# Block 0's rows and the queries' weights in two transfers each, biases turned by a plain matmul, outputs in new PSUM places, more tiles added in chunks 1 and 3

## The chip, the core and the metric

One core of a Trainium2 chip runs the whole program. Its engines work side by side, each through its own list of instructions: TensorE (PE, with its weight loads as PEld), VectorE (DVE), ScalarE (ACT), GpSimd (POOL) and SyncE (SP), which here only issues transfers. The metric is the device time of one execution in microseconds (us).

## What is computed

For x of 2048 rows and 640 columns, a layer norm without weights, and then two branches whose results are added to x: attention with 32 heads of 20 columns, where each row attends to itself and to seven earlier rows, two apart; and a dense layer of 1536 columns with gelu.

```python
def _A_ref(x, wqkv, wo):
    ...
    H = 32; Dh = D // H
    W, dil = 8, 2
    ...
    idx = pos[:, None] - off[None, :]
    mask = idx >= 0
    ...
    logits = jnp.einsum("bhsd,bhswd->bhsw", q, kg) * scale
    logits = jnp.where(mask[None, None, :, :], logits, -1e9)
    attn = _softmax(logits, axis=-1)
    o = jnp.einsum("bhsw,bhswd->bhsd", attn, vg)
    return ... @ wo
def _B_ref(x, w1, b1, w2, b2):
    h = _gelu(x @ w1 + b1)
    return h @ w2 + b2
xn = _layernorm(x)
return x + _A_ref(xn, A_wqkv, A_wo) + _B_ref(xn, B_w1, B_b1, B_w2, B_b2)
```

The second function is written here with `@` in place of its einsums.

## The kernel before

The rows are handled in four chunks (n = 0 to 3) of 512, each of four blocks (bl) of 128. A chunk's normalised rows are turned so that columns lie on the partitions (tile xnT). From it TensorE makes queries, keys and values (L336, in chunk 0 L349 and L380 in pieces) and the dense layer's first product (L599, tile hps), which ACT turns into hT with gelu (L615). Every product's PSUM tile comes from a pool of four banks (psA), two banks (psO) or the one place for the logits (psL, tile L).

Attention runs on VectorE. Queries times the eight shifted keys fill two big tiles, half 0 and half 1 (L433, four instructions a chunk). Each head's 20 columns lie as 4 partitions by 5 tiles; the sum over partitions is done by TensorE (L479, tile L) by a product with a 0/1 matrix, and the sum over the 5 tiles either by accumulating products in L479 or, in part, by adds on VectorE first (L465 adds pairs of tiles, L470 one tile to the first). LEVEL says how much per chunk: at 0 L479 runs 40 times, at 1 24, at 2 16, at 3 8. Then come mask (L490, chunk 0 only), maximum (L510), subtraction (L516), exponential on ACT (L526), sum (L530), reciprocal by logarithm and exponential on ACT (L538, L539), and the product with it (L544, tile attn). SP spreads attn over the partitions by transfers (L563, tiles ax or parts of x_sb), VectorE multiplies it with the shifted values (L578, eight a chunk) and adds up (L587, L592) to tile oT.

Chunks 0 to 2 leave turned: TensorE adds w2 x hT and wo x oT into tile T (L673, five slices s of 128 columns), ACT adds the bias (L676), SP turns the slice back by a transposing transfer (L680), and POOL adds it to the output in memory by an accumulating transfer (L685). Chunk 3 leaves straight, a block of rows at a time: the first 512 columns in tile lo, the other 128 in hi (L634, L636). Its blocks 0 to 2 go by ACT's copies (L641, L642) and accumulating transfers of POOL (L646); the last block is added to x by VectorE (L693, L702) and written by SP (L694) and ACT (L707). The x rows that the accumulating transfers add to were written to the output before (L301, L305).

The order is written out by hand, as one long list of names (ORDER), and each name issues a few instructions on its engines. TensorE, VectorE, ACT and SP carry out theirs exactly in that order; POOL's order follows the program too. Names: pj and pc are a projection and its copy, f1 and ge the dense product and gelu, qk L433, pa L465, pb L470, lg L479, m, mx, ex, ss, ri, at the softmax steps, xd and xs the transfers of attn, av L578, ad L587, ot L592, t a part of T, u L676, ut L680, ud L685, o the parts of lo and hi, oc and od copies and transfers of a block of chunk 3, oclo L693 with L694, ohi the hi products of the last block, ochi L702, ochd L707. The digits behind are chunk, then block or slice, then part. At the end the list reads

```
... u24 o312 ut23 o313 ud22 ud23 ot3 o320 o321
o322 o323 o324 oc32 od32 ut24 o314 oc31 od31 o300 o301 o302 o303 o304 o332 o333 o334 ud14 ohi ud24 oc30 od30 oclo ochi
ochd
```

At the start SP loads block 0 of x (L129), then the weights of queries and keys (L132), blocks 2 and 3, the values' weights and chunk 1, while ACT's queue loads block 1 and the biases (L136 to L138); ACT makes block 1's statistics (L221, L228), VectorE those of the other blocks (L209, L211). Thirteen products without use (L446) keep TensorE busy until the first transposes (L280). The two bias vectors are laid in 17 rows of a tile of 32 (b_rt) and turned by a transpose (L456, L459).

Of the kernel before, what the change touches and what calls it, by code (L numbers as in the profile page):

```python
# [11 lines left out]
ALU = mybir.AluOpType  # L12
# [17 lines left out]
LASTB = S // P - 1  # L30
WARM = 10
RB = 32
# [3 lines left out]
LEVEL = (1, 0, 2, 2)  # L36
# [6 lines left out]
tp01a gb3 tp01b tc01a tc01b gb4 gd gc0 ge tb b1 hj102 gc1 ho st02a st02 st03a hc102 gc4 st03 hj101 rs02 xn02 rs03 xn03  # L43
st10a st12a st13a st11a hc101 st12 hj100 hc100 hj200 tp02 tc02 tp03 tc03 pk st13 hj201 hc200 st11 st10 hj202 hc202
hj012 hc012 hc201 rs1 rc1 hj112 hc112 xn12 tc12 xn10 hj210 qk000 hj011 hc011 tc10 hj110 hc110 qk001 hj010 hc010 hc210
hj111 hc111 qk011 qk010 pa011 pa001 xn11 tc11 xn13 hj211 hc211 f10_5 tc13 f10_4 ge0_4 ge0_5 f10_0 ge0_0 f10_7 f10_10
pj113 pc113 pj103 pj111 ge0_10 pj101 pc111 pj114 ldx ge0_7 pa000 pc101 pa010 lg0 mask m0a ld2 pc103 pj102 pc114 pad11
su21 mx0a ex0a pj112 pc112 m0b mx0b ss0a pc102 ex0b ri0a ss0b pj100 pc100 at0a ri0b at0b pj110 pj104 pc104 pc110 xd0
qk111 f10_2 ge0_2 su22 qk100 hj212 hc212 f10_6 ge0_6 pj121 su20 f10_1 pc121 su23 ldo f11_10 ge1_10 ng2 ge0_1 sq20
f11_5 f10_11 pj122 pc122 f10_3 qk110 sq22 t040 qk101 f11_0 t000 lg1 xp0 av010 ge0_3 sq21 xs0 ge1_0 sq23 rs2 f10_8  # L50
ge0_8 t001 m1 f11_3 rc2 xn23 tc23 ge0_11 av031 t041 mx1 av021 xn20 tc20 f11_7 av011 ge1_5 ge1_7 av001 ge1_3 xp1 f10_9
t042 t002 xn21 ge0_9 tc21 pj120 xn22 tc22 av030 av000 f11_9 ge1_9 pj124 ex1 av020 ss1 pc120 pc124 pj123 pc123 ad00 ri1
t043 f11_2 t003 pj204 at1 pc204 xd1 su31 ad01 pad12 ad02 ot0 pj200 pc200 pj201 pc201 av101 xp2 pj212 su30 pc212 pj220
pj213 pc220 pc213 pj223 pc223 pj211 su33 pc211 pj203 su32 ng3 sq33 pad21 av100 sq31 pj202 f11_6 t004 u00 av110 xs1
av130 t044 av120 av131 av121 t010 av111 t011 t012 t013 u04 t020 t014 sq32 pc203 pc202 pj221 sq30 rs3 rc3 ad11 u01 ut00
ad10 ad12 t030 pj210 pc221 t031 t021 t022 ut01 ge1_2 pj214 xn33 tc33 t032 t033 t034 xn31 tc31 ge1_6 pj224 t023 t024
f11_8 ot1 pc214 pad22 pc210 qk201 qk211 qk210 xn30 tc30 f12_9 qk200 f11_1 pa210 pa201 xn32 ge1_8 u02 pa211 pa200 f11_4
ge1_1 t100 ge1_4 tc32 pj311 pc311 pb212 ud00 ud01 ge2_9 pj310 pc310 pad31 pj304 pc304 pj314 pc314 t101 pj300 pj324
pc324 ut02 pj303 f12_10 pb202 pc224 u03 pc303 xp3 pj301 pc301 xl ge2_10 pc300 f13_9 pj313 pc313 pj312 ud02 ut03 ud03
pj302 pc302 f13_6 ge3_6 pj323 lg2 pc312 qk300 m2 pc323 f11_11 ge1_11 f13_0 ge3_0 mx2 ut04 f13_11 ge3_9 ex2 pa300 ss2  # L60
qk310 ri2 at2 xs2 qk301 t130 t131 f12_1 ge2_1 ge3_11 t132 f13_10 qk311 t102 t103 f13_2 pa310 xd2 t104 pj320 pc320
f13_1 ge3_1 u10 ut10 ud10 f12_8 pa311 pa301 pb312 ge2_8 f13_8 ge3_8 t110 t133 t111 t112 t113 t114 u11 ge3_10 f12_5
pj222 pc222 pj321 pc321 pb302 lg3 av200 t134 u13 m3 av221 ge2_5 xb3 f12_11 t140 t141 t120 ut11 mx3 f12_2 ge3_2 av211
ex3 ss3 ri3 av220 ge2_2 f13_5 ge2_11 t142 t143 t121 t122 t123 f12_6 ge2_6 at3 xs3 f12_3 ge2_3 t124 u12 f12_7 pj322
ud04 av210 av201 av231 f12_0 t144 ge2_7 ge2_0 t200 av230 pc322 u14 ut12 ud11 f12_4 ge2_4 ge3_5 f13_4 ge3_4 o310 f13_7
ge3_7 t210 ad20 ad21 ad22 ot2 f13_3 t201 t202 pad32 av321 t203 ge3_3 o311 av331 ut13 av320 xd3 t204 u20 av300 ut14
ut20 ud12 ud13 t211 t212 t240 t213 t214 av311 u21 ud20 t241 t242 av310 av330 t220 t221 t222 t223 t224 u22 ut21 t243
av301 ad30 ad31 o330 o331 t230 ad32 t231 t232 t233 t234 u23 ut22 ud21 t244 u24 o312 ut23 o313 ud22 ud23 ot3 o320 o321
o322 o323 o324 oc32 od32 ut24 o314 oc31 od31 o300 o301 o302 o303 o304 o332 o333 o334 ud14 ohi ud24 oc30 od30 oclo ochi
ochd  # L70
# [4 lines left out]
def kernel(  # L75
# [45 lines left out]
    b_rt = consts.tile([RB, P], BF16, name="b_rt")  # L121
# [12 lines left out]
    load_x(0, 1)  # L134
    nc.vector.memset(x_sb[:, 1, 0:16], 0.0)
# [3 lines left out]
    load_w(0)  # L139
    load_w(1)  # L140
    load_x(2, BPC)
    load_w(2)
    load_x(BPC, 2 * BPC)
# [151 lines left out]
    def rows(n):  # L295
        cs = slice(n * BPC, min((n + 1) * BPC, LASTB))
        return cs, out_sd.rearrange("(b p) d -> p b d", p=P)[:, cs, :]
# [9 lines left out]
    def do_xl():  # L307
        nc.vector.tensor_tensor(out=x_sb[:, LASTB, :], in0=x_sb[:, LASTB, :], in1=b2bc[:], op=ALU.add)

# [144 lines left out]
    def do_tb():  # L454
        tiles["tb"] = psL.tile([P, 2 * W * P], BF16, tag="L", name="tb")
        nc.tensor.transpose(tiles["tb"][:, 0:RB], b_rt[:], ident[0:RB, 0:RB])  # L456

    def do_b1():
        nc.vector.tensor_copy(bT[:], tiles["tb"][:, 0 : FT + KT])  # L459
# [39 lines left out]

    def shifted(n, i):  # L500
        cs, width = part(n, i)
        if PARTS[n] == 1:
            return tiles["L", n][:]
        low = half[0][:].rearrange("p w t c -> p (w t c)").bitcast(F32)[:, 0 : W * P]
        return low.rearrange("p (i w c) -> p i w c", i=PARTS[n], w=W)[:, i, :, :]
# [22 lines left out]
    def do_sum(n, i):  # L528
        total = softmax_tile("sums", n, [P], F32)
        nc.vector.tensor_reduce(  # L530
            out=total[:, i, :], in_=tiles["e", n][:, i, :, :].rearrange("p w c -> p c w"), axis=AX.X, op=ALU.add
        )

    def do_recip(n, i):
        rs = get(("rs", n), lambda: smp.tile([P, PARTS[n], P // PARTS[n]], F32, tag="m", name="rs"))
        total = tiles["sums", n][:, i, :]
        table(LOG_SET)
        nc.scalar.activation(total, total, ACT.Ln)  # L538
        nc.scalar.activation(rs[:, i, :], total, ACT.Exp, scale=-1.0)  # L539

    def do_attn(n, i):
        cs, width = part(n, i)
        attn = get(("attn", n), lambda: smp.tile([P, W, P], BF16, tag="attn", name="attn"))
# [76 lines left out]
    def do_o(n, bl, pc, parts):  # L620
        cs = slice(bl * P, (bl + 1) * P)
        if pc == 0 and "lo" in parts:
            for part in ("lo", "hi"):
                pool, tag = (psA, "acc") if bl % 2 else (psO, "o")
                tiles[part, n, bl] = pool.tile([P, CH], F32, tag=tag, name=part)
        lo, hi = tiles["lo", n, bl], tiles["hi", n, bl]
# [4 lines left out]
        for k, (lhs, rhs) in enumerate(srcs):  # L631
            first, last = pc == 0 and k == 0, pc == 4 and k == len(srcs) - 1
            if "lo" in parts:
                nc.tensor.matmul(lo[:], lhsT=lhs, rhs=rhs[:, 0:CH], start=first, stop=last)  # L634
            if "hi" in parts:
                nc.tensor.matmul(hi[:, 0 : D - CH], lhsT=lhs, rhs=rhs[:, CH:D], start=first, stop=last)  # L636
# [211 lines left out]
```

## Time and profile before

| what | us |
| --- | --- |
| median of 3 runs (lowest to highest) | 210.02 (209.96 to 210.23) |
| the profiled execution, its own time | 210.03 |
| its span, first to last instruction | 208.0 |
| PE, DVE, ACT busy between 18 and 194 us | 175.5, 169.1, 113.0 |
| PE, DVE, ACT busy after 194 us | 10.8, 1.0, 2.3 |

The span is what the profiler saw of the program; the execution took 2.0 us more. The busy times of the stretches show that TensorE and VectorE are both nearly full in the middle, and that VectorE has no more work in the last 14 us. A row of a group gives line, engine, operation, what is written and read, shapes and count, and then busy time, mean length in ns and the idle time before. A row of the timeline begins with start and length; in brackets stands the idle time before it and what ended it. The clock granted to TensorE was 0.999 of full speed.

### The profile page before, as it was taken

The page shows a single profiled execution, that of the slowest core. Times are in us where ns is not written, and L with a number is a line of the kernel's source. Part 1 is how long each engine was busy: PE and PEld are TensorE (multiplying, and loading weights), DVE is VectorE, ACT ScalarE, POOL GpSimd, SP SyncE. Part 2 cuts the span into 40 slices and gives each one's busy share as a digit, 9 for nine tenths or more (in the row PEclk, how much of TensorE's full clock was granted, in tenths as well). Part 3 has the DMA queues.
Part 4 walks back from the last instruction along what each step waited for, and adds up shares of the span by engine and source line. Part 5 has one row for each costly group of instructions (what it writes and reads, how often), then busy time and mean ns, then how long its engine had stood idle before and what let it go on. Part 6 is the DMA issues. An engine that isn't in the chain of part 4 may idle for free.

```text
span 208.0 us, 2951 instructions
## 1 busy us (share of the span) xinstructions
PE 203.5 (98%) x1164; PEld 107.0 (51%) x1164; DVE 180.9 (87%) x141; ACT 127.5 (61%) x234; POOL 24.9 (12%) x37
## 2 busy tenths in 40 slices
PE   8999999999999999999999999999999999999993
PEld 3999754554445554444455544444444444445552
DVE  2598995999699999999999989999999999999201
ACT  5589968898997877877564556744658541112210
POOL 2000000000000000220020610002200402222621
PEclk9999999999999999999999999999999999999999
DMA  6994379168426075148431790086405795556753
GB/s 217 388 395 137 68 207 395 60 122 238 162 82 162 11 189 138 25 50 91 90 25 56 114 123 0 0 188 81 37 0 100 121 108 54 50 50 76 49 68 63
DMA packets 36863, 23.88 MB, mean 115 GB/s; under 512 B 24946, under 2 KB 34674, under 8 KB 36850
## 3 DMA queue, kind: packets, MB, share of 16 engines
q1 hardware_dynamic: 26320, 18.75, 34.5%
q0 software_dynamic: 8752, 2.95, 17.8%
q10 hardware_dynamic: 1778, 2.00, 2.7%
q8 instruction: 9, 0.15, 0.3%
q14 instruction: 4, 0.03, 0.0%
HBM read 10.00 MB, written 5.57 MB: 75 GB/s over the span
## 4 chain that ended last, share of the span: by engine, by line
PE 66%; DVE 21%; ACT 9%; DMA 2%; issue 1%; DVEq 0%; ACTq 0%
PE T L673 17%; PE pps L336 15%; PE hps L599 13%; PE lo L634 7%; PE gps L380 7%; DVE half L433 5%; DVE half L587 4%; DVE sums L530 3%; PE idle L446 2%; ACT L173 2%; DVE half L465 2%; DMA xnT<-xn 2%; DVE half L578 2%; ACT hT L615 2%; PE hi L636 2%; PE gps L349 1%
## 5 line engine op out<-in xcount | busy, mean ns | idle before, releaser
L599 PE MATMUL hps<-xnT,w_sb 128*128 128x512 bf16 x240 | 56.9, 379 | 0.1
L433 DVE TENSOR_TENSOR half<-qT,kT 128x5120 bf16<-128x5120 bf16 x16 | 44.3, 2820 | 1.0 <-ACT vT L400 0.7
L673 PE MATMUL T<-hT,w_sb 128*128 128x512 bf16 x180 | 43.3, 379 | 0.0
L685 POOL DMA_DIRECT2D out_dram<-x_sb x15 | 19.5, 1357 | 172.8 <-DMA x_sb<-x_sb 168.7
L599 PEld LDWEIGHTS <-w_sb 128*128 128x128 bf16 x240 | 23.3, 98 | 28.2 <-issue 1.2
L615 ACT ACTIVATE hT<-hps,bT 128x512 bf16<-128x512 f32 x36 | 24.1, 687 | 7.3 <-PE hps L599 7.2
L673 PEld LDWEIGHTS <-w_sb 128*128 128x128 bf16 x180 | 17.6, 98 | 21.1
L578 DVE TENSOR_TENSOR half<-vT,ax 128x2560 bf16<-128x2560 bf16 x16 | 23.1, 1484 | 2.4 <-PE L L479 2.4
L676 ACT ACTIVATE x_sb<-T,bT 128x512 bf16<-128x512 f32 x15 | 10.3, 687 | 23.6 <-PE T L673 23.6
L578 DVE TENSOR_TENSOR half<-vT,x_sb 128x2560 bf16<-128x2560 bf16 x16 | 22.6, 1485 | 0.0
L587 DVE TENSOR_TENSOR half<-half,half 128x5120 bf16<-128x5120 bf16 x8 | 22.3, 2820 | 0.1
L673 PE MATMUL T<-oT,wo 128*128 128x512 bf16 x75 | 18.3, 379 | 0.3 <-DVE oT L592 0.3
L336 PE MATMUL pps<-xnT,wk_sb 128*128 128x512 bf16 x75 | 18.3, 379 | 0.0
L336 PE MATMUL pps<-xnT,wv_sb 128*128 128x512 bf16 x75 | 18.3, 379 | 0.0
L336 PE MATMUL pps<-xnT,wq_sb 128*128 128x512 bf16 x75 | 18.2, 379 | 0.0
L173 ACT ACT_TABLE_LOAD x12 | 15.4, 1283 | 0.9 <-PEq L832 0.7
L465 DVE TENSOR_TENSOR half<-half 128x2048 bf16<-128x2048 bf16 x12 | 13.9, 1217 | 0.0
L336 PEld LDWEIGHTS <-wv_sb 128*128 128x128 bf16 x75 | 8.8, 117 | 7.6
L336 PEld LDWEIGHTS <-wq_sb 128*128 128x128 bf16 x75 | 8.7, 118 | 7.7 <-issue 0.4
L336 PEld LDWEIGHTS <-wk_sb 128*128 128x128 bf16 x75 | 8.8, 117 | 7.5
L263 ACT ACTIVATE xn<-x_sb,nmr,rstd 128x640 bf16<-128x640 bf16 x12 | 10.6, 916 | 3.2 <-DMA xnT<-xn 2.3
L400 ACT CAST vT<-pps 128x512 bf16<-128x512 f32 x15 | 8.5, 589 | 6.1 <-PE pps L336 6.1
(92 smaller groups left out, 241.0 us busy)
## 6 DMA issues: line engine op xcount, KB each, us to landing
w_sb<-in_B_w_dram SPq DMA_DIRECT2D x4, 960.0 KB, 10.3
ax<-attn SPq DMA_DIRECT2D x8, 256.0 KB, 4.8
x_sb<-attn SPq DMA_DIRECT2D x8, 256.0 KB, 4.6
out_dram<-x_sb POOLq DMA_DIRECT2D x15, 128.0 KB, 4.0
x_sb<-in_A_x_dram SPq DMA_DIRECT2D x1, 1280.0 KB, 6.5
out_dram<-x_sb ACTq DMA_DIRECT2D x2, 640.0 KB, 3.1
wq_sb<-in_A_wqkv_dram SPq DMA_DIRECT2D x1, 800.0 KB, 4.7
wk_sb<-in_A_wqkv_dram SPq DMA_DIRECT2D x1, 800.0 KB, 6.3
```

Source lines behind the costliest of these rows:

```text
L173: nc.scalar.preload_act_table_set(name)
L336: nc.tensor.matmul(ps[:], lhsT=wqkv_p[which][:, ti, to, :], rhs=xnT[:, ti, :], start=(ti == 0), stop=(ti == KT - 1),)
L380: nc.tensor.matmul(ps[:, to - a, :], lhsT=wqkv_p[which][:, ti, to, :], rhs=tiles["xnT", 0][:, ti, pair * 2 * P : (pair + 1) * 2 * P], star ...
L433: nc.vector.tensor_tensor(out=half[h][:, :, :, cs], in0=q[:, :, at].unsqueeze(1).to_broadcast([P, W // 2, KT, 2 * P]), in1=window(k, h, at ...
L465: nc.vector.tensor_tensor(out=even, in0=even, in1=odd, op=ALU.add)
L578: nc.vector.tensor_tensor(out=half[h][:, :, :, cs], in0=window(qkv_tile(n, 2), h, cs), in1=ax_view(n)[:, j, ws, :].unsqueeze(2).to_broadca ...
L587: nc.vector.tensor_tensor(out=a, in0=a, in1=b, op=ALU.add)
L599: nc.tensor.matmul(ps[:], lhsT=w1_sb[:, ti, ft * P : (ft + 1) * P], rhs=tiles["xnT", n][:, ti, :], start=(ti == 0), stop=(ti == KT - 1),)
L615: nc.scalar.activation(hT, tiles["hps", n, ft][:], ACT.Gelu_apprx_tanh, bias=bT[:, ft : ft + 1], scale=1.0)
L634: nc.tensor.matmul(lo[:], lhsT=lhs, rhs=rhs[:, 0:CH], start=first, stop=last)
L673: nc.tensor.matmul(ps[:], lhsT=lhs, rhs=rhs, start=pc == 0 and k == 0, stop=pc == 4 and k == len(srcs) - 1)
L685: nc.gpsimd.dma_start(dst, src, accum_op=ALU.add)
```

## The change

- Block 0 of x is loaded in two halves of 320 columns, one on SP's and one on ACT's queue; the queries' weights in two transfers, of two and of three of the five row tiles; blocks 2 and 3 now come before the keys' weights, and chunk 1 before the values'.
- The tile b_rt has 128 rows, and a plain product with the identity turns the biases.
- LEVEL is 1 in place of 0 for chunk 1, and 3 in place of 2 for chunk 3.
- The sum of the softmax is made by three halving adds, in f32, in a free part of half 0 or of attn.
- In chunk 3, block 0 and the hi parts of blocks 0 and 1 use the place of the logits; the hi parts of blocks 2 and 3 share a bank. Block 2 too is added to x by VectorE and written by SP (new names dc and dd), and the rows written beforehand are fewer by one block.
- ORDER is a new list throughout. In chunk 0 the first two L433 are followed by their adds; chunk 1 has its pa100 pa110 pa101 pa111, chunk 3 its pb304 and pb314.

Its end reads now

```
... ot3 u24 o321 o322 o323 o313 o314 o304 oc31 oc30 o324 o333 ut22 ud22 o334 dc oclo ut23 ut24 ud23
ohi od31 od30 dd ud24 ochi ochd
```

and the rest of the diff, cut to its core (its last two lines stand near the top of the kernel):

```diff
-LEVEL = (1, 0, 2, 2)
+LEVEL = (1, 1, 2, 3)
+DIRECT = 2
...
-    load_x(0, 1)
-    nc.vector.memset(x_sb[:, 1, 0:16], 0.0)
+    for eng, cs in ((nc.sync, slice(0, D // 2)), (nc.scalar, slice(D // 2, D))):
+        eng.dma_start(x_sb[:, 0, cs], x_nb[:, 0, cs])
     nc.scalar.dma_start(x_sb[:, 1, :], x_nb[:, 1, :])
     nc.scalar.dma_start(b_rt[0:FT, :], B_b1.rearrange("(t p) -> t p", p=P))
     nc.scalar.dma_start(b_rt[FT : FT + KT, :], B_b2.rearrange("(t p) -> t p", p=P))
-    load_w(0)
+    for ts in (slice(0, 2), slice(2, KT)):
+        nc.sync.dma_start(wqkv[0][:, ts, :], wqkv_v[:, ts, 0:D])
+    load_x(2, BPC)
     load_w(1)
-    load_x(2, BPC)
+    load_x(BPC, 2 * BPC)
     load_w(2)
-    load_x(BPC, 2 * BPC)
...
     def do_xl():
-        nc.vector.tensor_tensor(out=x_sb[:, LASTB, :], in0=x_sb[:, LASTB, :], in1=b2bc[:], op=ALU.add)
+        rows_ = x_sb[:, LASTB + 1 - DIRECT :, :]
+        nc.vector.tensor_tensor(
+            out=rows_, in0=rows_, in1=b2bc[:].unsqueeze(1).to_broadcast([P, DIRECT, D]), op=ALU.add
+        )
...
     def do_tb():
-        tiles["tb"] = psL.tile([P, 2 * W * P], BF16, tag="L", name="tb")
-        nc.tensor.transpose(tiles["tb"][:, 0:RB], b_rt[:], ident[0:RB, 0:RB])
+        tiles["tb"] = psL.tile([P, W, P], F32, tag="L", name="tb")
+        nc.tensor.matmul(tiles["tb"][:, 0, 0 : FT + KT], lhsT=b_rt[:], rhs=ident[:, 0 : FT + KT], start=True, stop=True)
 
     def do_b1():
-        nc.vector.tensor_copy(bT[:], tiles["tb"][:, 0 : FT + KT])
+        nc.vector.tensor_copy(bT[:], tiles["tb"][:, 0, 0 : FT + KT])
...
+    scratch = half[0][:].rearrange("p w t c -> p (w t c)").bitcast(F32)
...
+    def sums(n, i):
+
+        if PARTS[n] == 1:
+            return attn_tile(n)[:].rearrange("p w c -> p (w c)").bitcast(F32).rearrange("p (w c) -> p w c", w=W // 2)
+        room = scratch[:, W * P : W * P + W * P // 2]
+        return room.rearrange("p (i w c) -> p i w c", i=PARTS[n], w=W // 2)[:, i, :, :]
...
     def do_sum(n, i):
-        total = softmax_tile("sums", n, [P], F32)
-        nc.vector.tensor_reduce(
-            out=total[:, i, :], in_=tiles["e", n][:, i, :, :].rearrange("p w c -> p c w"), axis=AX.X, op=ALU.add
-        )
+        a, e = sums(n, i), tiles["e", n][:, i, :, :]
+        nc.vector.tensor_tensor(out=a, in0=e[:, 0 : W // 2, :], in1=e[:, W // 2 :, :], op=ALU.add)
+        for k in (2, 1):
+            nc.vector.tensor_tensor(out=a[:, 0:k, :], in0=a[:, 0:k, :], in1=a[:, k : 2 * k, :], op=ALU.add)
...
-        total = tiles["sums", n][:, i, :]
+        total = sums(n, i)[:, 0, :]
...
+    def out_ps(bl, hi):
+        first = lambda: psL.tile([P, W, P], F32, tag="L", name="tail")
+        if bl == 0 or (hi and bl == 1):
+            ps = get("tail", first)[:].rearrange("p w c -> p (w c)")
+            return ps[:, CH + bl * P : CH + (bl + 1) * P] if hi else ps[:, 0:CH]
+        key = "hi" if hi else ("lo", bl)
+        pool, tag = (psO, "o") if key == ("lo", BPC - 1) else (psA, "acc")
+        ps = get(key, lambda: pool.tile([P, CH], F32, tag=tag, name="hi" if hi else "lo"))
+        return ps[:, (bl - BPC + DIRECT) * P : (bl - BPC + DIRECT + 1) * P] if hi else ps[:]
...
+    def do_o(bl, pc, parts):
+        n, cs = NCH - 1, slice(bl * P, (bl + 1) * P)
...
         for k, (lhs, rhs) in enumerate(srcs):
-            first, last = pc == 0 and k == 0, pc == 4 and k == len(srcs) - 1
+            final = pc == 4 and k == len(srcs) - 1
             if "lo" in parts:
-                nc.tensor.matmul(lo[:], lhsT=lhs, rhs=rhs[:, 0:CH], start=first, stop=last)
+                nc.tensor.matmul(out_ps(bl, False), lhsT=lhs, rhs=rhs[:, 0:CH], start=pc == 0 and k == 0, stop=final)
             if "hi" in parts:
-                nc.tensor.matmul(hi[:, 0 : D - CH], lhsT=lhs, rhs=rhs[:, CH:D], start=first, stop=last)
-
-    def do_oc(n, bl):
+                bank = bl // 2
+                first = bank not in opened
+                opened.add(bank)
+                nc.tensor.matmul(
+                    out_ps(bl, True), lhsT=lhs, rhs=rhs[:, CH:D], start=first, stop=final, skip_group_check=True
+                )
...
+    def direct(bl, hi):
+
+        b = (NCH - 1) * BPC + bl
+        room = half[1][:].rearrange("p w t c -> p (w t c)")[:, (bl % 2) * D : (bl % 2 + 1) * D]
+        cs = slice(CH, D) if hi else slice(0, CH)
+        nc.vector.tensor_tensor(out=room[:, cs], in0=out_ps(bl, hi), in1=x_sb[:, b, cs], op=ALU.add)
+        return room, out_sd[b * P : (b + 1) * P, :]
...
+    def do_dc():
+        direct(BPC - 2, False)
+        tiles["dc"] = direct(BPC - 2, True)
+
+    def do_dd():
+        room, dst = tiles["dc"]
+        nc.sync.dma_start(dst, room)
 
     def do_oclo():
-        osb = outp.tile([P, D], BF16, tag="osb", name="osb")
-        tiles["osb", last] = osb
-        nc.vector.tensor_tensor(out=osb[:, 0:CH], in0=tiles["lo", *last][:], in1=x_sb[:, LASTB, 0:CH], op=ALU.add)
-        nc.sync.dma_start(out_sd[LASTB * P :, 0:CH], osb[:, 0:CH])
+        room, dst = direct(BPC - 1, False)
+        nc.sync.dma_start(dst[:, 0:CH], room[:, 0:CH])
...
     def do_ochi():
-        osb = tiles["osb", last]
-        nc.vector.tensor_tensor(
-            out=osb[:, CH:D], in0=tiles["hi", *last][:, 0 : D - CH], in1=x_sb[:, LASTB, CH:D], op=ALU.add
-        )
+        tiles["hi"] = direct(BPC - 1, True)
...
     def do_ochd():
-        nc.scalar.dma_start(out_sd[LASTB * P :, CH:D], tiles["osb", last][:, CH:D])
+        room, dst = tiles["hi"]
+        nc.scalar.dma_start(dst[:, CH:D], room[:, CH:D])
 
...
-    b_rt = consts.tile([RB, P], BF16, name="b_rt")
+    b_rt = consts.tile([P, P], BF16, name="b_rt")
```

## The prediction

> **What bounds the kernel now.** I read the page's busy times first, then the groups by shape, VectorE's timeline, the chain of waits, and last the queues of SP and POOL.
>
> ```profile
> PE 203.5 (98%) x1164; PEld 107.0 (51%) x1164; DVE 180.9 (87%) x141; ACT 127.5 (61%) x234; POOL 24.9 (12%) x37
> L479 PE MATMUL L<-half,head_of 128*32 128x512 bf16 x96 | 5.9, 381 | 0.2 <-DVE half L470 0.2
> L530 DVE TENSOR_REDUCE sums<-e 128x128 f32<-128x1024 bf16 x3 | 5.8, 1917 | 0.3 <-ACT e L526 0.3
> L516 DVE TENSOR_TENSOR half<-L,m 128x512 f32<-128x512 f32 x2 | 1.4, 692 | 0.1
> ```
> TensorE is never idle for long, so it sets the end, and only fewer products, fewer stalls or a shorter tail can help. The other three rows are prices used below.
>
> ```profile
> 17.77 11.03 DVE L433 TENSOR_TENSOR half<-qT,kT 128x5120 bf16<-128x5120 bf16 x4
> 28.72 4.62 DVE L465 TENSOR_TENSOR half<-half 128x2048 bf16<-128x2048 bf16 x4
> 35.63 0.29 DVE L490 TENSOR_TENSOR L<-L,mask 32x128 f32<-32x128 f32 x1 [2.29 <-PE L L479]
> 54.97 1.49 DVE L578 TENSOR_TENSOR half<-vT,ax 128x2560 bf16<-128x2560 bf16 x1 [1.69 <-PE L L479]
> 192.27 1.49 DVE L592 TENSOR_TENSOR oT<-half 128x2560 bf16<-128x2560 bf16 x1
> 203.95 0.69 DVE L693 TENSOR_TENSOR osb<-lo,x_sb 128x512 bf16<-128x512 f32 x1 [10.19 <-PE lo L634]
> ```
> From 17.77 to 193.76 (192.27 + 1.49) VectorE is full too, with 6.0 us of gaps, of which two stand here. The last attention tile (oT) is ready at 193.76, and TensorE uses it from 193.99: both engines are balanced, and about 10.8 us of products follow.
>
> ```profile
> 34.17 1.41 PE L L479 x24
> 172.86 10.36 PE T L673 x48
> 203.86 0.96 PE hi L636 x17
> 204.84 0.29 DVE osb L702
> ```
> These are lines of the chain: a 128x512 product every 0.216 us (10.36 / 48), one of L479 every 0.058 (1.41 / 24), a 128x128 every 0.056 (0.96 / 17). After the last product comes 3.2 us of tail to the span's end at 208.0.
>
> ```profile
> 164.42 27.08 SPq L680 DMA_TRANSPOSE x_sb<-x_sb  x6
> 204.67 0.35 SPq L694 DMA_DIRECT2D out_dram<-osb  x1
> SPq L694 <- DVE osb L693: 13.1, 1, 13.1
> L680 SPq DMA_TRANSPOSE x_sb<-x_sb x15: 1189/1194/3732, 83.8 to 190.3; - x15
> L685 POOL DMA_DIRECT2D out_dram<-x_sb x15: 1282/1285/1838, 86.8 to 193.8; - x15
> DMA to landing us min/median/max: 3.7/4.0/7.5
> ```
> SP stood still for 13.1 us at the output transfer L694, until VectorE had written its source. It cost nothing: the last transpose had been issued at 190.3. The last row is that of L685, from issue to landing.
>
> **The change, part by part.**
>
> *Products of L479.* Adding tiles in chunk 1 takes 40 of them to 24, in chunk 3 16 to 8: 24 fewer x 0.058 = 1.4 us off TensorE.
>
> *VectorE's price.* Chunk 1 gains four L465 at 1.14 (starts 28.72 to 33.34 for four): +4.6. Chunk 3 gains two L470 of the same size: +2.3. Five sums become three halving adds each. For 1024 elements these are of 512, 256 and 128. No row adds bf16 into f32; by L516 (692 ns for 512, 1228 for 1024: 1.05 ns an element and 156 fixed) they take 0.69 + 0.42 + 0.29 = 1.40, less overlap 1.27, against starts 1.86 apart. The lower bound is 1.0, were the first add as fast as L465 (0.52 ns an element), the upper the 1.92 of the reduction. I take 1.27, since L516 also writes f32: -0.6 for each of three, -0.2 for each of the two small ones. The doubled row add costs +0.3. Sum: about +5.0 us. The Trainium skill (VectorE: DVE Perf Modes, "What auto-detection actually checks") says that the doubled rate needs every tensor to be 16-bit, so it puts the first add at the slow rate, as I do; at the fast rate VectorE would win another 0.3 per sum, off the path.
>
> *Start.* Block 0's rows come in halves on SP and ACT. The left half may land earlier than 3.26, but block 1's rows are now second on ACT's queue: 0.24 later, and ACT sums them (3.62 to 4.45) before block 0's rstd (4.49). So the first transpose (5.46) goes 0.2 later; if the halves win, 0.2 earlier, not more, since the warm-up products fill TensorE to 5.26. I take +0.2. The Trainium skill speaks against the split too (DMA: Bandwidth & Descriptors, "Issuing engines are not separate DMA queues"): several issuing engines save only the time of issue, so by it the halves win nothing here. The queries' weights have 0.3 us to spare now (landing 5.9, first product 6.25), and their first part comes earlier. The keys' weights move behind rows 2 and 3: 1.12 MB had landed at 5.9 and 3.68 MB at 12.46, so 0.39 MB/us, and 2.24 MB land at 8.8; the first product is at 9.5. The rows of chunk 1 land at 10.4 instead of 12.46. VectorE's statistics thus follow without a gap, and its first L433 starts near 15.9 instead of 17.77: 1.9 us back. The plain matmul for the biases costs nothing: like the 0.12 us transpose it stands between other products; the zeroing of 128 rows runs on POOL before.
>
> *Where the two engines meet.* TensorE's times are counted as slots (0.216, 0.109 for 256 columns by L380's 9.28 / 85, 0.056, 0.058) from the first transpose on. VectorE's are starts in order (L433 2.74, L465, L470, L510 and L516 1.14, L578 1.40, L587 2.8), or the length that the same stretch had before.
> - L of chunk 0: VectorE is ready at 15.9 + 4 x 2.74 + 4 x 1.14 = 31.4; TensorE is there from 31.7 to 33.1, so the mask starts at 33.3 (35.63 before).
> - L of chunk 1: 33.3 + 6.4 (softmax, 6.6 before) + 10.9 + 4.6 = 55.2; TensorE is there at 55.0 and reads half 0 first (12 x 0.058), so L578 starts at 55.9 (54.97 before).
> - oT of chunk 0: seven L578, L510 and L516 to 68.0; the sum, an L578 and attn to 71.8; three L587, L578 and L592 to 83.0 (81.72 before). TensorE wants it at 83.4; before it waited 0.4 there.
> - L of chunk 2: 83.0 + 37.6 (39.0 before, less an L578 done already) = 120.6; TensorE 120.9, L433 at 121.6 (121.94).
> - L of chunk 3: 121.6 + 23.1 as before + 2.3 - 0.6 = 146.4; TensorE 146.9, L578 at 147.3 (145.92).
> - last oT: 147.3 + 47.8 as before - 0.6 (sum) - 0.2 (its wait for e) = 194.3; TensorE wants it at 194.9.
>
> So the 5 us of extra VectorE work is paid by 1.9 at the start and by gaps, and TensorE waits nowhere for long. The slots of all its products sum to 197.1 (788 of 512 columns, 125 of 256, 141 of 128, 96 of L479), against 199.4 between 5.46 and 204.82: 2.3 were stalls, of which 0.7 (start, end of the pipeline) stay. Gain: 1.4 + 1.6 - 0.2 for the start, less 0.4 for stalls that margins of 0.3 to 0.6 will let through (0.3 to 0.5 each where they came before): 2.4 us. The last block's low products, ahead of L636's 17, end at 203.70 - 2.4 = 201.3, the last product at 202.4. The new PSUM places add no wait: the bank of L is free once chunk 3's exponential is done, near 153, and the first output product there comes at 162.
>
> *The tail.* This decides. In the order written out, chunk 2's transposes 23 and 24 now stand **behind** the last block's output transfer on SP (ut23 ut24 after oclo; before, both went first). SP will hold at that transfer as at L694, and with it both transposes, and POOL's last two accumulating transfers (ud23, ud24). From 201.3: VectorE starts 0.25 later (203.95 after 203.70), 0.69 for the add, 0.4 for the transfer's issue: 202.6. First transpose at 202.7, the second 1.32 later (188.98 and 190.30 before) at 204.0; landing takes 2.3 to 2.7, so 205.2 and 206.5. POOL: first transfer 205.25 to 206.53, second from 206.55, landing 3.9 later (3.7 to 4.0) at 210.45. From the last landing to the span's end it was 1.3 (206.66 to 207.97): 211.75. Block 2's direct write (two adds in place of ACT's copies and a POOL transfer) stands behind the last transpose on SP and lands by 207.
>
> The profiled execution took 210.03 for its span of 208.0 (2.03 around it), as good as the median 210.02. 211.75 + 2.03 = 213.8; the last landings come with nearly nothing beside them, where the medians are from busier stretches, so I say **213.6**: 3.6 slower, although TensorE ends 2.4 earlier.
>
> **The rivals.**
> *Faster: the transposes are not held.* If they go as soon as ACT has written their source (near 192, as before), the tail of 3.2 follows products that end at 202.4: span 205.6, time 207.6. For it: no row shows a transpose behind an output transfer. Against: SP's waits of 52.1 us for attn, with transposes behind them in its order. It decides if the last transpose is issued before 197.9, since 2.5 + 3.9 + 1.3 after that is 205.6.
> *Slower still: VectorE is late.* If the f32 adds cost what the reduction did (0.6 each) or L578 waits for ax, the last oT comes 1 to 3 us later; what exceeds the margin of 0.6 goes to the end: 2.4 late gives 215.4. For it: small margins at six meeting points in a row. Against: before, the same kind of margin let only 0.3 to 0.5 through at a time.
> *No change.* TensorE would have to end 3.6 earlier still, 6.0 in all, where its stalls and the 24 products together hold 3.7: 210.0.
>
> **How the numbers follow.** 0.72 for the forecast, 0.14 for VectorE late, 0.10 for faster, 0.04 for no change. The forecast's own range goes from 212.4 (no stall let through, start unchanged, landings of 2.3 and 3.7) to 215.1 (gain of 0.9 only). The range, 212.0 to 215.6, takes in 0.4 less after the last landing and most of the late case. About 0.2% is what a measurement of this kernel can tell from no change. Faster 0.10, same 0.04, slower 0.86.
>
> **What would show it.** Right: SP's transfer of the last block issued near 202, two transposes after it, POOL's last two transfers after 205 and the last landing near 210, with TensorE done near 202. L479's count 72, the first L433 near 16, the mask near 33. Wrong: the last transpose issued before 197; TensorE's last product after 204; a VectorE gap over 1 us before a product of L578.

## The result: 6.0 us slower, by the held transposes and by block 1's rows

Measured beside each other, the changed kernel takes 216.01 us in the median of 4 runs (215.89 to 216.24), the kernel before 209.99 (209.90 to 210.23): a ratio of 1.0286, interval 1.0268 to 1.0304. Predicted were 213.6, in a range of 212.0 to 215.6. The direction and the main cause are as predicted; the forecast is 2.4 us short, and the time lies 0.4 above its range.

The profiled execution of the changed kernel took 216.24 us, with a span of 214.2. First its end, in the chain that ended last (start, length, what):

```profile
203.25 0.70 DVE half L680
203.97 0.35 SPq L733
...
204.41 2.32 DMA x_sb<-x_sb
...
206.77 0.50 issue
207.28 0.86 POOL out_dram L720
208.13 0.65 issue
208.79 1.32 POOLq L879
```

The last block's sum (L680) at 203.25, its output transfer on SP (L733), and only then the first transpose (204.41). POOL starts its accumulating transfer 0.5 us after that has landed. The timeline of SP and POOL shows the rest:

```profile
204.41 2.58 SPq L715 DMA_TRANSPOSE x_sb<-x_sb  x2
...
207.28 1.30 POOL L720 DMA_DIRECT2D out_dram<-x_sb  x1 [4.79 <-DMA x_sb<-x_sb]
208.81 1.30 POOL L720 DMA_DIRECT2D out_dram<-x_sb  x1 [0.23 <-issue]
```

Two transposes, two transfers, the last landing at 212.65 (an L720 takes 3.8 from issue to landing). TensorE was done at 204.16, so 10 us of the span follow its last product; before the change it was 3.2.

The second loss is at the start. First the kernel before (L136 there is block 1's rows, L221 their sum on ACT, L280 the first transpose):

```profile
0.91 0.39 ACTq L136 DMA_DIRECT2D x_sb<-in_A_x_dram  x1
...
3.62 0.74 ACT L221 ACTIVATE trash<-x_sb 128x640 bf16<-128x640 bf16 x1 [1.59 <-DMA x_sb<-in_A_x_dram]
...
5.46 0.39 PE L280 MATMUL tp<-ident,xn 128*128 128x128 bf16 x2
```

Then the changed kernel, its timeline and the DMA issues of the first 16 us (the last figure is the time from issue to landing):

```profile
1.19 0.46 ACTq L136 DMA_DIRECT2D x_sb<-in_A_x_dram  x1
1.21 0.93 SPq L140 DMA_DIRECT2D wq_sb<-in_A_wqkv_dram  x2
...
5.34 0.74 ACT L222 ACTIVATE trash<-x_sb 128x640 bf16<-128x640 bf16 x1 [1.36 <-DMA x_sb<-in_A_x_dram]
...
6.08 0.28 ACT L246 ACTIVATE logv<-mv,eps_t 128x1 f32<-128x1 f32 x1
...
7.03 0.28 PE L281 MATMUL tp<-ident,xn 128*128 128x128 bf16 x2 [1.54 <-DVE xn L266]
```

```profile
x_sb<-in_A_x_dram ACTq DMA_DIRECT2D x1, 160.0 KB, 4.1
x_sb<-in_A_x_dram SPq DMA_DIRECT2D x1, 80.0 KB, 2.3
x_sb<-in_A_x_dram ACTq DMA_DIRECT2D x1, 80.0 KB, 2.4
```

The two halves of block 0's rows land at 3.0 and 3.2, hardly ahead of the whole (3.24 before). Block 1's rows, issued at 1.19, need 4.1 us and land at 5.32 (issued at 0.91, they landed at 3.59 before). ACT sums them (L222) ahead of block 0's rstd (L246), so block 0 waits too: TensorE idles for 1.54 us, and its first transpose is at 7.03 instead of 5.46.

VectorE, for the prediction's meeting points:

```profile
17.30 5.55 DVE L437 TENSOR_TENSOR half<-qT,kT 128x5120 bf16<-128x5120 bf16 x2
...
34.95 0.29 DVE L494 TENSOR_TENSOR L<-L,mask 32x128 f32<-32x128 f32 x1 [2.09 <-PE L L483]
...
69.88 0.69 DVE L544 TENSOR_TENSOR attn<-e 128x512 f32<-128x512 bf16 x1
70.60 0.75 DVE L546 TENSOR_TENSOR attn<-attn 128x256 f32<-128x256 f32 x2
71.27 1.48 DVE L592 TENSOR_TENSOR half<-vT,ax 128x2560 bf16<-128x2560 bf16 x1
...
195.53 1.49 DVE L606 TENSOR_TENSOR oT<-half 128x2560 bf16<-128x2560 bf16 x1
```

The last oT is ready at 197.0 (193.8 before), yet TensorE never waited for it: the list of what PE waited for holds only the first transpose and the first product.

```profile
PE tp L281 <- DVE xn L266: 1.5, 1, 1.5
PE idle L450 <- PEq L868: 0.8, 1, 0.8
```

### The profile page after: what moved, and what is told of

The parts are those of the page before. It is cut to its first block, busy times and chain, and to the rows that moved or that the text cites. A ratio compares the mean times of both kernels' runs of the same rounds, so it can differ in the third digit from the quotient of the medians.

```text
span 214.2 us, 2935 instructions
## 1 busy us (share of the span) xinstructions
PE 201.8 (94%) x1140; PEld 106.0 (50%) x1140; DVE 186.6 (87%) x158; ACT 128.9 (60%) x234; POOL 24.0 (11%) x36
## 3 DMA queue, kind: packets, MB, share of 16 engines
q10 hardware_dynamic: 1794, 1.92, 2.5%
## 4 chain that ended last, share of the span: by engine, by line
PE 92%; DMA 3%; issue 1%; POOLq 1%; DVE 0%; POOL 0%; ACT 0%; ACTq 0%; SPq 0%
PE T L708 26%; PE hps L613 24%; PE pps L340 23%; PE gps L384 6%; PE lo L656 5%; PE L L483 2%; DMA x_sb<-in_A_x_dram 2%; PE tail L656 2%; PE gps L353 1%; DMA x_sb<-x_sb 1%; PE tail L661 1%; PE tp L281 1%; POOLq L879 1%; PE hi L661 0%; POOL out_dram L720 0%
## 5 line engine op out<-in xcount | busy, mean ns | idle before, releaser
L437 DVE TENSOR_TENSOR half<-qT,kT 128x5120 bf16<-128x5120 bf16 x16 | 44.5, 2821 | 0.8 <-ACT vT L404 0.5
L708 PE MATMUL T<-hT,w_sb 128*128 128x512 bf16 x180 | 43.9, 379 | 0.0
L720 POOL DMA_DIRECT2D out_dram<-x_sb x15 | 19.5, 1381 | 171.0 <-DMA x_sb<-x_sb 170.4
L469 DVE TENSOR_TENSOR half<-half 128x2048 bf16<-128x2048 bf16 x16 | 18.8, 1219 | 0.0
L340 PE MATMUL pps<-xnT,wk_sb 128*128 128x512 bf16 x75 | 17.8, 379 | 0.0
L340 PE MATMUL pps<-xnT,wq_sb 128*128 128x512 bf16 x75 | 17.7, 379 | 0.0
L404 ACT CAST kT<-pps 128x512 bf16<-128x512 f32 x15 | 8.7, 588 | 5.7 <-PE pps L340 5.6
L404 ACT CAST qT<-pps 128x512 bf16<-128x512 f32 x15 | 8.7, 584 | 5.7 <-PE pps L340 5.7
```

The source lines that it names most:

```text
L340: nc.tensor.matmul(ps[:], lhsT=wqkv_p[which][:, ti, to, :], rhs=xnT[:, ti, :], start=(ti == 0), stop=(ti == KT - 1),)
L404: nc.scalar.copy(dest[:, to, off : off + CH], tiles["pps", n, which, to][:])
L437: nc.vector.tensor_tensor(out=half[h][:, :, :, cs], in0=q[:, :, at].unsqueeze(1).to_broadcast([P, W // 2, KT, 2 * P]), in1=window(k, h, at ...
L469: nc.vector.tensor_tensor(out=even, in0=even, in1=odd, op=ALU.add)
L708: nc.tensor.matmul(ps[:], lhsT=lhs, rhs=rhs, start=pc == 0 and k == 0, stop=pc == 4 and k == len(srcs) - 1)
L720: nc.gpsimd.dma_start(dst, src, accum_op=ALU.add)
```

## The experiments

Every run is compared with the kernel before, timed on the same chip beside it. Two questions stood: does the order on SP make the tail, and what at the start delays block 1's rows? A theory for the start was that these rows, issued 0.28 us later, now share the DMA engines with the queries' weights.

**The tail alone: e1_tail_first and e5_old_tail_held.** The first takes the changed kernel and moves four names in ORDER:

```
-... ut22 ud22 o334 dc oclo ut23 ut24 ud23 ohi od31 od30 dd ud24 ochi ochd
+... ut22 ud22 ut23 ud23 ut24 ud24 o334 dc oclo ohi od31 od30 dd ochi ochd
```

> The changed kernel with only the order at its end altered: chunk 2's last two transposes (ut23, ut24) and their accumulating transfers (ud23, ud24) stand ahead of the last block's add and output transfer (oclo). Theory (the transposes are held on SP behind oclo's output transfer): they are issued before 195, the last landing is that of the output transfers near 206.3 where it was 212.65, and the time is 209.5 us (216.0 less 6.5). TensorE's end stays where it was, near 203.9. Rival (the late transposes are not what sets the end; POOL's transfers are late for another reason): the last of POOL's landings stays after 210 and the time at 215 to 216.

Measured: 210.34 us (10 runs, 209.50 to 211.27), ratio 1.002, interval 0.9996 to 1.0044. The timeline of SP and POOL at its end:

```profile
187.42 8.60 SPq L715 DMA_TRANSPOSE x_sb<-x_sb  x3
...
197.69 1.28 POOL L720 DMA_DIRECT2D out_dram<-x_sb  x1 [4.05 <-DMA x_sb<-x_sb]
```

The last transpose is issued by 196.0 (194.83, a little inside the bound expected), POOL's last L720 at 197.7, and the span ends at 207.8 with TensorE done at 204.04. The runs lie in two groups, 209.5 to 209.9 and 210.8 to 211.3; the first is the expected value. In four of the second five TensorE's mean granted clock is 0.990 or 0.991, where the first five have 0.996 to 1.0; the last section comes back to that. So 5.7 us of the change are the order on SP.

The second does the reverse to the kernel before:

```
-... u24 o312 ut23 o313 ud22 ud23 ot3 ... oc32 od32 ut24 o314 ... ud14 ohi ud24 oc30 od30 oclo ochi ochd
+... u24 o312 o313 ud22 ot3 ... oc32 od32 o314 ... ud14 ohi oc30 od30 oclo ut23 ut24 ud23 ud24 ochi ochd
```

> The kernel before with one thing altered: its last two transposes (ut23, ut24) and their accumulating transfers (ud23, ud24) stand behind the last block's add and output transfer (oclo), as in the changed kernel. Theory (the held transposes are the whole tail, whatever else was changed): after the low products' end at 203.7 come 11.2 us, as in the changed kernel (203.04 to 214.2), so the span is 214.9 and the time 216.9 us, 6.9 more. Rival (the tail needs other parts of the change, such as block 2's direct output on SP): less than 4 more.

Measured: 216.96 us (216.87 to 217.25), ratio 1.033, interval 1.0313 to 1.0347. Its timeline is that of the changed kernel, 0.8 us later:

```profile
204.71 0.35 SPq L694 DMA_DIRECT2D out_dram<-osb  x1
...
205.18 2.58 SPq L680 DMA_TRANSPOSE x_sb<-x_sb  x2
...
208.08 1.30 POOL L685 DMA_DIRECT2D out_dram<-x_sb  x1 [4.63 <-DMA x_sb<-x_sb]
209.60 1.30 POOL L685 DMA_DIRECT2D out_dram<-x_sb  x1 [0.22 <-issue]
```

The tail needs nothing else of the change: four names in another place cost the kernel before 6.9 us.

**The start: e2_x_whole and e3_sum_second.** Both keep the changed kernel's tail. The first undoes the halves:

```
-for eng, cs in ((nc.sync, slice(0, D // 2)), (nc.scalar, slice(D // 2, D))):
-    eng.dma_start(x_sb[:, 0, cs], x_nb[:, 0, cs])
+load_x(0, 1)
```

> The changed kernel with one part undone: block 0's rows again in one transfer on SP, so that block 1's rows are first on ACT's queue. The queries' weights stay in two transfers. Theory (block 1's rows land late because they are issued 0.28 us later, level with the first part of the queries' weights, and share the DMA engines with it): they land near 3.6 (5.32 in the changed kernel), the first transpose is at 5.5 (7.03), and the time is 214.5 us, 1.5 less. Rival A (the weights' two transfers or their place delay the rows): they still land after 5, and the time stays at 216. Rival B (the lost time at the start is made up by later waits): the first transpose is at 5.5, but the time falls by less than 0.5.

Measured: 216.29 us (215.93 to 216.30), ratio 1.0289, interval 1.0259 to 1.0318: nothing gained, and none of the three accounts is whole. Block 1's rows do land early (issued 0.74, landed 3.75), and the first transpose moves to 5.81. But the second part of the queries' weights, issued at 1.67, lands at 8.11 (6.61 in the changed kernel), TensorE waits 0.96 for it, and block 1's first transpose stays at 8.47 (8.65). The theory named the right transfer and overlooked the next one.

The second exchanges two instructions on ACT:

```
-... st00a st00 sum1 rs00 mean1 neg1 ...
+... st00a st00 rs00 sum1 mean1 neg1 ...
```

> The changed kernel with two instructions on ACT exchanged: block 0's rstd (rs00) ahead of block 1's sum (sum1), so that block 0 does not wait for block 1's rows. Theory (block 1's rows themselves are what TensorE waits for, since its transposes of block 1 follow 1.2 us of products after those of block 0): the first transpose moves to 5.5, but block 1's first transpose only from 8.65 to about 8.2; TensorE stands before it, and the time falls by 0.4 to 215.6 us. Rival (it is only the order on ACT that holds the start): the time falls by 1.5, to 214.5 us.

Measured: 216.49 us (215.63 to 217.54), ratio 1.0295, interval 1.0238 to 1.0351: no gain over the changed kernel that can be measured, and the rival's 214.5 lies outside the interval (its lower end is 215.0). The first transpose moved only to 6.53, since VectorE has block 1's mean1 ahead of xn00a. In the profiled execution block 1's first transpose came at 8.88, later instead of earlier, because TensorE's clock had dropped to half after the wait (last section); the two runs with a mean clock of 0.988 and 0.989 took 215.63 and 215.82, the theory's value. What holds the start is block 1's rows, more than the order on ACT.

**Both: e4_tail_whole.** The edits of e1 and e2 together.

> Both of the edits before (transposes ahead at the end, block 0's rows whole). Theory (the two losses lie in series and add): 208.0 us, 1% faster than the kernel before. Rival (the start's gain is absorbed by VectorE's extra adds later on, once TensorE is earlier): 209 to 209.5 us.

Measured: 209.84 us (10 runs, 209.30 to 210.69), ratio 0.9991, interval 0.9972 to 1.0011. It is the rival's number, not for the rival's reason: the queries' second part landed at 8.40 again and block 1's first transpose was at 8.76, so there was no gain at the start for VectorE to absorb. That put the split of the weights under suspicion.

**The weights whole: e6_tail_both_whole.** As e4, and

```
-for ts in (slice(0, 2), slice(2, KT)):
-    nc.sync.dma_start(wqkv[0][:, ts, :], wqkv_v[:, ts, 0:D])
+load_w(0)
```

> The run with transposes ahead and block 0's rows whole (209.84 us), with the queries' weights in one transfer too; the new order of rows and weights behind them stays. Theory (the weights' second part, issued at 1.67 and landed at 8.1 to 8.4 there, is what the split of the weights costs): whole, they land near 5.9 as before, block 1's first transpose is at 7.4 (8.5 in all four runs so far), and the time is 208.7 us. Rival (the DMA engines are slow from 4 to 6 because both blocks' rows are issued at 0.74): the weights land after 7 and the time stays at 209.3 to 209.8.

Measured: 208.87 us (208.82 to 209.10), ratio 0.9944, interval 0.9929 to 0.9959: as expected, and faster than both kernels. The weights land at 6.07, and the timeline reads

```profile
1.20 0.42 SPq L132 DMA_DIRECT2D wq_sb<-in_A_wqkv_dram  x1
...
5.89 0.28 PE L279 MATMUL tp<-ident,xn 128*128 128x128 bf16 x2 [1.28 <-DVE xn L264]
...
7.50 0.29 PE L279 MATMUL tp<-ident,xn 128*128 128x128 bf16 x2
...
16.14 5.56 DVE L435 TENSOR_TENSOR half<-qT,kT 128x5120 bf16<-128x5120 bf16 x2
```

VectorE's first L435 is at 16.14, where the prediction had put it (15.9).

**The halves with whole weights: e8_tail_wq_whole.** As e6, but with block 0's rows in two halves on two queues.

> Transposes ahead, block 0's rows in two halves as changed, the queries' weights in one transfer. Theory (block 1's rows are late because they are issued behind a half of block 0's rows and level with the weights): they still land after 5, block 1's first transpose stays near 8.5, and the time at 209.9 us or more. Rival (the split of the weights is the whole loss): the rows land before 4.3, block 1's first transpose is at 7.4, and the time is 208.7.

Measured: 212.65 us (210.82 to 213.11), ratio 1.0106, interval 1.006 to 1.0151. Block 1's rows, issued at 1.21, landed at 5.86, the first transpose was at 7.56. Against e6, one edit apart, the halves cost 3.8 us. In the profiles 1.7 of that is the later first transpose (7.56 for 5.89); from it to the last product TensorE then takes 199.5 us, 2.4 more than in e6, because its products come at half the rate until about 13 us. The last section comes back to that.

**On the old kernel: e11_old_x_split.** The kernel before with the halves, and without the 16 columns written first.

> The kernel before with one thing altered: block 0's rows in two halves on SP and ACT, and the 16 columns not written first. Theory (the halves alone make block 1's rows late): they land after 5, block 1's first transpose moves from 7.1 to 8.6 or later, and the time rises by 1.5 us to 211.5, since TensorE makes up nothing. Rival (the kernel before had stalls that absorb it, for its VectorE waits for chunk 1's rows until 16.4 in any case): 210.5 or less.

Measured: 213.12 us (211.44 to 213.65), ratio 1.013, interval 1.0085 to 1.0175: it absorbs nothing, and loses twice what was expected. Block 1's rows landed at 6.16, the first transpose was at 7.87, and TensorE's clock dropped after its wait of 2.70. The one run of the four with a mean clock of 1.0 took 211.44, the theory's value; the three at 0.992 took 212.7 to 213.7. So, by that one run, 1.3 of the 3.0 is the late rows and the rest goes with the dropped clock.

**Is it the halves or the place? e12_halves_on_sp.** As e6, with two halves on SP:

```
-load_x(0, 1)
+for cs in (slice(0, D // 2), slice(D // 2, D)):
+    nc.sync.dma_start(x_sb[:, 0, cs], x_nb[:, 0, cs])
```

> The fastest version so far (transposes ahead, queries' weights whole) with block 0's rows in two halves again, but both on SP, so that block 1's rows stay first on ACT's queue. Theory (it is the place and the moment of issue of block 1's rows that cost, not the halves): they land before 4, the first transpose stays within 0.3 of 5.89, and the time is 208.9 us; the weights, issued 0.4 later, land near 6.3. Rival (the halves' smaller packets slow the DMA engines at the start): block 1's rows or the right half land after 4.3, the first transpose is after 6.3, and the time is 209.4 or more.

Measured: 210.15 us (10 runs, 209.60 to 212.33), ratio 1.0026, interval 0.9993 to 1.006. The places are the theory's: block 1's rows land at 3.42, the first transpose is at 5.54. The time is not: the queries' weights, issued 0.46 later than in e6 (1.66 for 1.20), landed 1.8 later, at 7.86, and TensorE waited 1.63 for them. So block 1's rows are late because of where and when they are issued, not because block 0's come in halves; no run parts the place (second on ACT's queue) from the moment (level with the weights). What a later issue does to the weights is a cost of its own.

**The new order of the loads: e7_tail_old_start and e10_best_first.** e7 has e1's order at the end and all loads as before the change; e10 is e6 with one line back in front of ACT's transfers. The two differ by the order of the loads alone (minus: e7, plus: e10):

```
 load_x(0, 1)
 nc.vector.memset(x_sb[:, 1, 0:16], 0.0)
...
 load_w(0)
-load_w(1); load_x(2, BPC); load_w(2); load_x(BPC, 2 * BPC)
+load_x(2, BPC); load_w(1); load_x(BPC, 2 * BPC); load_w(2)
```

> Transposes ahead, and all loads at the start as before the change: block 0's rows whole, the 16 columns written first, the queries' weights whole, the keys' weights ahead of rows 2 and 3. Theory (the start's loss lies in the loads alone): block 1's rows land at 3.6, the queries' weights at 5.9, block 1's first transpose is at 7.1 as before, and the time is 208.4 us. Rival (the new order of the pieces needs rows 2 and 3 earlier): VectorE's statistics wait for rows 2 and 3 (landing at 8.8) and chunk 1's rows (12.5), its first L433 starts after 17.5, and the time is 209 or more.

> The fastest version so far with the 16 columns of block 1's rows written first again, as before the change, which holds ACT's first transfer from 0.74 to 0.91. Theory (block 0's rows, alone at first, land near 3.2 rather than 3.67, and what follows shifts with them): the first transpose is at 5.45 (5.89) and the time 208.4 us. Rival (block 1's rows or the weights' landing at 6.1 hold what follows): block 1's first transpose stays at 7.5 and the time at 208.9.

Measured: e7 210.51 us (10 runs, 209.92 to 211.76), ratio 1.0027, interval 1.001 to 1.0043; e10 208.95 (208.61 to 209.10), ratio 0.9943, interval 0.9929 to 0.9958. In e7 the rival is right: rows 2 and 3 land at 9.41, their statistics start at 9.44, TensorE waits 1.1 for their rstd, and VectorE's first product of queries and keys starts at 18.02. The new order of rows and weights is worth 1.6 us. In e10 the steps came as the theory says (first transpose 5.46, last product 202.57, span 206.5, each 0.4 to 0.5 earlier than in e6), and yet the time did not fall: 2.3 to 2.5 us lie around the span in its four runs, 1.9 to 2.1 in e6's. That was so in nine of e7's ten runs too (2.4 to 2.5). Both have the 16 columns written first, but so has the kernel before, with 2.03. The cause stays open.

**Which engine bounds? e9_less_adds.** e6 with LEVEL as before the change, so that chunk 1 is not added up before L483's products and chunk 3 one step less (`pa100 pa101 pa110 pa111 pb304 pb314` leave ORDER).

> The fastest version so far (transposes ahead, rows and queries' weights whole, 208.87 us) with chunks 1 and 3 added as before the change (LEVEL 1, 0, 2, 2): 24 products of L479 come back to TensorE, and some 6.9 us of additions leave VectorE. Theory (TensorE bounds from its first transpose on: last product less first transpose is 197.13, 197.11 and 197.11 us in the changed kernel and two of these runs): 24 x 0.058 = 1.4 us more, 210.2 us. Rival (VectorE bounds, since its first L433 and the last product shift by the same 1.16 us between two of these runs): the time falls, to 208.5 or less.

Measured: 210.47 us (10 runs, 210.20 to 212.08), ratio 1.0012, interval 0.9987 to 1.0037. From its first transpose (5.86) to its last product (204.18) TensorE takes 198.3 us, 1.2 more than in e6, of the 1.4 expected; and VectorE, with some 7 us less to do, stands and waits:

```profile
DVE nmr L252 <- ACT rstd L247: 4.1, 1, 4.1
...
DVE half L590 <- PE L L481: 3.5, 1, 3.5
```

TensorE bounds, and the added tiles are worth 1.6 us to the kernel that has nothing else wrong.

## Where the prediction was right, and the step that failed

The prediction's span was 211.75, the measured one 214.2: 2.45 to account for.

- **The step that failed is the start.** "So the first transpose (5.46) goes 0.2 later": it went 1.57 later, to 7.03. The prediction saw that block 1's rows are second on ACT's queue and that ACT sums them before block 0's rstd. It priced this as 0.24 us of issue, as if a transfer issued 0.24 later landed 0.24 later. Issued 0.28 later, second on its queue and level with the weights, the rows landed 1.7 later. Every run with them issued at 1.19 to 1.21 (e1, e3, e8, e11, the changed kernel) had them land between 5.18 and 6.16; every run that issued them at 0.74 or 0.91 (the kernel before, e2, e4 to e7, e9, e10, e12) between 3.4 and 3.9. This is 1.37 of the 2.45, and the largest part. With both splits undone (e6 against e1) the median falls by 1.5 us (1.0 against the faster half of e1's runs), and TensorE's last product comes 1.04 earlier in the profiles. The queries' weights, counted as "0.3 us to spare", were not in the way in the changed kernel, but were when block 1's rows came early (e2, e4, e12).
- **The tail was right, and 0.71 too short.** From the end of the last block's low products to the span's end it took 11.16 us (203.04 to 214.2) for 10.45 predicted. POOL's first transfer started 0.55 after the transpose had landed, not 0.05; the trace of before showed such a gap (landing 192.49, POOL 193.02), and the sum left it out. The second came 0.2 later than back to back, the end 0.26 later after the last landing (1.56 for 1.3), and the transpose landed 0.2 sooner than said.
- **TensorE.** From first transpose to last product 197.1 us, 2.2 less than before: predicted were 2.6. That is the remaining 0.37. The 72 products of L483 are there (4.6 us busy, x72), and the list of waits names none after the first transpose, so the waits of before (0.3 for oT, 0.2 for L470) are gone, as said. Still 197.1 is 1.4 above the slots that the prediction counted (its 197.1 less the 24 products), where its sum left 1.1; where the difference sits the list does not show. e9 shows by an edit that the 24 products are worth their price.
- **VectorE's price did not reach the end**, as forecast, though every meeting point came later than listed: first L437 at 17.30 (15.9 said), mask at 34.95 (33.3), last oT at 197.0 (194.3). About half of that is the start: in e6 the first products of all four chunks on VectorE and the last product on TensorE come 1.16 us earlier than in the changed kernel, together. In e6 the three points stand at 16.14, 33.80 and 195.87, so the prediction's own stretches came out 1.6 short by the last oT; TensorE never waited for it, so it cost nothing. The sum of 1024 elements took 1.39 from start to start (69.88 to 71.27; 1.27 said, within 1.0 to 1.92). The first add, bf16 in and f32 out, took 0.69 us: the slow rate, as the Trainium skill says (VectorE: DVE Perf Modes, "What auto-detection actually checks"), and the trace agrees.
- **The halves win nothing**: the Trainium skill's rule (DMA: Bandwidth & Descriptors, "Issuing engines are not separate DMA queues") says that issuing from several engines saves only the time of issue. The halves landed 0.06 to 0.24 us before the whole had. The rule held. The loss came from the transfer that the split pushed back, not from the halves.
- **The rivals.** "The transposes are not held" fell with SP's timeline and with e5. "VectorE is late" names 215.4, nearer to the measured 216.01 than the forecast, but by coincidence: the last oT did come 2.7 later than listed, yet TensorE never waited for it, and with less for VectorE to do (e9) the time rose. Without the hold and with the start mended, e6 came to 208.87; the faster rival, with its 207.6, had counted on the predicted TensorE end and 3.2 us of tail. e6 ended at 203.0 and 4.0 after it.

So the change has two parts that help (the order of rows and weights 1.6 us, e10 against e7; the added tiles 1.6, e6 against e9) and three that hurt: the transposes behind the output transfer, 5.7 (e1); the halves on two queues, 3.8 with whole weights (e8 against e6), of which some 2.4 are TensorE's slow start there; with split weights 0.5 (e1 against e4), which is not shown, as the two intervals overlap; the split of the queries' weights, 1.0 once the rows are whole (e4 against e6). The plain matmul for the biases and block 2's direct output were not tried alone; both stand in the fastest version, so what each is worth stays open.

## What to carry to other kernels

A queue that issues in order turns one late transfer into the time of all that stand behind it: before moving anything on it, list what is behind, and follow that to the last landing. At the start, where everything is asked for at once, look at what is ahead of a transfer on its queue and what is issued level with it, and do not price it by the delay of its issue: 0.28 us later in the queue was 1.7 us later in memory here. And sum a chain from the gaps that the trace shows between its links (here 0.5 from landing to start on POOL), not only from the links.

## What the runs showed of the hardware

*How late the weights land is not a matter of bytes alone.* In e12 the same 1.1 MB (blocks 0 and 1 and the queries' weights) landed 1.8 us later than in e6, after the weights' issue had moved by 0.46. The DMA view of the first 16 us (GB/s in slices of 0.4 us), e6 and then e12:

```profile
GB/s 0 0 0 0 58 102 278 353 375 390 397 384 378 387 387 381 390 394 397 394 394 397 394 394 394 397 390 400 397 394 399 399 399 403 403 429 373 380 388 384
```

```profile
GB/s 0 0 0 0 80 104 368 262 61 71 243 323 378 330 301 294 339 371 394 381 381 387 394 400 390 394 397 394 390 400 394 397 397 396 407 398 399 407 392 407
```

In e12 the rate falls to 61 and 71 GB/s from 3.2 to 4.0, about when the rows land (3.42), and then stays under 380 until 7.2. The changed kernel and e8 have such holes too (102 and 61 GB/s from 2.8), e2 a shallower one (200 from 4.0); the kernel before, e6 and e10 stay at 290 or more from 2.8 on. Why the holes come, and why the rate stays low behind them, was not settled.

*TensorE's clock drops after a short pause.* In e12 TensorE waited 1.63 us for the weights (6.3 to 7.9). The view by windows (the figure after the bracketed counts is the granted clock, before the DMA share and GB/s):

```profile
7.00:8.00 1.00, 0.09 (x1) 0.10 (x2) 0.38 (x2) 0.00 (x0) 0.00 (x0) 0.99 1.06 382
8.00:9.00 1.00, 1.00 (x11) 1.00 (x12) 0.00 (x0) 0.00 (x0) 0.00 (x0) 0.50 1.05 387
9.00:10.00 1.00, 1.00 (x12) 1.00 (x11) 0.05 (x1) 0.00 (x0) 0.00 (x0) 0.50 1.07 394
10.00:11.00 1.00, 1.00 (x13) 1.00 (x11) 1.00 (x4) 0.20 (x1) 0.00 (x0) 0.50 1.07 396
11.00:12.00 1.00, 1.00 (x17) 1.00 (x16) 0.96 (x4) 1.00 (x3) 0.00 (x0) 0.80 1.06 394
```

For over 3 us it runs at half the clock: 11 to 13 products per us, where the changed kernel has 20 to 22 at the same work. The same followed pauses of 1.92 (e3) and 2.70 (e11); the pause of 1.54 in the changed kernel's profile was not followed by it. Among the ten runs of e12 the four with a mean clock of 0.991 or 0.992 took 211.4 to 212.3 us, the others 209.6 to 210.3, so a drop costs about 2 us there. The Trainium skill (TensorE: Matmul & The Clock Gate, "What's actually happening") gives about 3.4 us for an idle window that halves the clock, in windows that run free of the kernel; here pauses of half that length were followed by it. Four of e1's ten runs show the same low mean clock, and e1's profiled pause is only 1.40, so no length near that is shown to be safe.

*e8 is another case.* There, too, products come at 12 to 13 per us behind a pause of 2.04, although the column of the clock says 1.00. But in e8 the products were at half the rate before the pause as well: the weight loads of the warm-up products (512 columns each) start 0.43 us apart up to the last ones at 5.0, twice the 0.216 of a later product. All profiles begin like that; in e6 the spacing shortens at 3.6, in e12 at 4.6. So in e8 the pause did not slow TensorE; it had not yet sped up, and did so only around 13 us. Whether the pause delayed that is not shown.
